# Attention feeding a two-layer network: the down-sampled pairs of later batches get shifted start times

## The chip, the core and the metric

The kernel runs on one NeuronCore of one Trainium2 chip. Five engines work from their own queues, each in program order: TensorE (PE in the profile; PEld is its weight load), VectorE (DVE), ScalarE (ACT), GpSimd (POOL) and SyncE (SP), which here only issues transfers. They wait for one another through semaphores. Matrix products land in PSUM, which has eight banks of 128 partitions by 512 float32 values. The metric is the device time of one execution in microseconds. The kernel before takes 1014.43 us, the median of three runs (1014.23, 1014.43 and 1015.88).

## The reference, cut to what matters

For 8 batches of 8 heads with 576 tokens of 64 values there are two attentions: one over tokens averaged by fours (144 of them), whose rows are repeated four times, and a local one in which a token sees only the tokens less than four places away. Their sum is the input of a network with 2048 hidden units.

```python
q_d, k_d, v_d = (z.reshape(B, H, Sd, 4, D).mean(axis=3) for z in (q, k, v))
out_up = np.repeat(sm_attn(q_d, k_d, v_d), 4, axis=2)
mask = np.abs(pos[:, None] - pos[None, :]) < 4
scores = np.where(mask, scale * (q @ k.T), -1e9)
attn_out = out_up + softmax(scores) @ v          # (8, 8, 576, 64)
x = attn_out.transpose(0, 2, 1, 3).reshape(4608, 512)
h = x @ w_in                                      # (4608, 2048)
out = (np.maximum(h, 0) + alpha * np.minimum(h, 0)) @ w_out
```

## The kernel before, in words

The network is the larger part. Its 4608 rows are cut into 18 chunks of 256, and the 2048 hidden units into 8 blocks of 256, which makes 144 steps. One step s is `hidden` (24 products into `h`, line 752), then `slopes` (two pairs of ACT operations, lines 760 and 761), `larger` (one DVE maximum, line 764) and `split` (ACT makes the upper part `gh`, line 769, POOL the rest `gl`, line 69), and then `product` (12 products into `o`, line 798). Operands stand as an upper and a lower part, so each product is made of three.

The attention of the first batch is worked out ahead of all that. The other seven batches run beside the network. Their local attention comes in units, three to a batch (u = 3 to 23), and is DVE work for the most part: `multiply` and `total` (lines 591 and 595), a softmax, then `weigh` and `gather` (lines 647 and 650). At the end of a unit, `flip` turns its result on PE (`xp`, line 659) in two parts, and `join` (DVE, line 671) reads that, adds the down-sampled result and so frees the bank; `place` makes the network's operands `xh` and `xl` of it.

The down-sampled attention comes in pairs of heads, four to a batch, each handled by one call of `down`. A pair is a chain on several engines. Its six inputs are loaded (`load`, line 232, through SP's queue into a ring of three tiles `ld`) and summed by fours (`fold`, line 238, POOL). Then `flip` turns the sums on PE (`qkT`, line 250); `operands` copies them out (ACT, `qd` and `kd`, lines 255 and 258); `scores` (PE, `s`, line 263); `peak` (DVE, `dnb`, line 267) and `exps` (ACT, `dp`, line 273); `invert` and `scale`; two `turn`s (PE, `pT`, line 287) with two `turned` (ACT, `th`, line 291); `weigh` (PE, `pv`, line 297) and `store` (ACT, `od`, line 302).

Five results of a pair (`qkT`, `s`, two `pT`, `pv`) and the two `xp` of a unit live in one PSUM pool of two banks, `bank("d")`, defined at line 62. A new one can be written only when the last reader of what stood in its bank is done. I call the time from the write to that last read a stay.

No scheduler orders the work. Each operation is entered with a due time counted in network steps (`at`), and all entries are sorted by that time; ties keep the order of entry. Step s enters `hidden` at s - 1.95, `slopes` at s - 1.45, `larger` at s - 1.15, `split` at s - 1.0 and `product` at s + 0.6. A pair that is entered with `t0` and a gap of 0.45 folds at t0, t0 + 0.45 and so on, and flips at t1 = t0 + 3.0; the rest follows at the offsets of line 312: operands at t1 + 0.5, scores at 1.0, peak at 1.6, exps at 1.7, the turns at 3.0, weigh at 4.0, store at 4.5. A unit u starts at begin[u], and units are 5.92 steps apart after the first few. Lines 891 to 894 enter the pairs of batches 2 to 7, evenly spread over three units of time. They come ahead of the units, whose flips depend on places inside their own lists. I write "pair 4_3" for batch 4, pair 3, "u11_1" for part 1 of unit 11, and h62 and p62 for `hidden` and `product` of step 62.

Of the kernel before, what the change touches and what calls it, by code (L numbers as in the profile page):

```python
# [16 lines left out]
B, H, S, D = 8, 8, 576, 64  # L17
# [33 lines left out]
def tile_attention_moe(ctx: ExitStack, tc: tile.TileContext, q, k, v, w_in, w_out, alpha, out):  # L51
# [514 lines left out]
    def local(u, t0, t1):  # L566
        b, jj = u // 3, u % 3
# [118 lines left out]
                at_ += n  # L686

        def put(i, t):
            at(t, join, i)
            at(t + 0.05, place, i, False)  # L690
            at(t + 0.3, place, i, True)
# [21 lines left out]
        t = t0  # L713
        when = {}
# [18 lines left out]
            at(when["total", str((1, 5, 2))] + 0.05, load_kv, u + 1, "k")  # L733
            at(t1 + 0.05, load_kv, u + 1, "v")
        if by_half:
            at(when["own"] - 0.6, flip, 0)
            put(0, when["own"])
        return when, put, flip


# [92 lines left out]
    with tc.tile_pool(name="start", bufs=1) as start:  # L833
        load_pair, load_windows, pair = first_batch(start)
        todo = [(w, fp) for fp in range(NP) for w in range(2)]
        for step in ORDER.split():
            kind, i = step[0], int(step[1])
# [16 lines left out]
        def at(t, f, *args):  # L854
            events.append((t, len(events), f, args))
# [19 lines left out]
    t = T0_DEC  # L875
# [7 lines left out]
    for p in range(4 * (B - 1)):  # L883
        b, hp = 1 + p // 4, p % 4
# [3 lines left out]
    begin = dict(UNITS)  # L888
    for u in range(len(UNITS) + 3, 3 * B + 1):
        begin[u] = begin[u - 1] + U_STEP  # L890
    for b in range(2, B):
        first, end = begin[3 * b - 2], begin[3 * b + 1]
        for hp in range(4):
            down(b, hp, first + (end - first - 0.5) * hp / 4 - (2.7 if b == 2 else 4.5), 0.45)
    at(3.3, load_q, 3)
    at(3.4, load_kv, 3, "k")
    at(decoded + 0.3, load_kv, 3, "v")
    at(decoded + 0.6, place_rest)
    put = None
    for u in range(3, 3 * B + 1):  # L900
        if u < 3 * B:
            when, *mine = local(u, begin[u], begin[u + 1])
        else:
            when = {"before 0": begin[u] + 0.8, "before 1": begin[u] + 1.2}
        if put and u - 1 in BY_HALF:
            at(begin[u] + 0.3, flip, 1)
            put(1, when["before 0"])
        elif put:
            at(begin[u] + 0.3, flip, 0)
            put(0, when["before 0"])  # L910
            t = when["before 0"] + 0.25 if u == 4 else when["before 1"]
            at(max(begin[u] + 0.31, t - 0.6), flip, 1)
            put(1, t)
        put, flip = mine
    with tc.manual_schedule():
        for _, _, f, args in sorted(events, key=lambda e: e[:2]):
            f(*args)
# [25 lines left out]
```

## Time and profile before

| what | value |
|---|---|
| median of three runs | 1014.43 us |
| the profiled execution | 1012.62 us |
| its span, first to last instruction | 1010.8 us |
| mean granted TensorE clock | 0.973 |
| DVE busy | 832.8 us (82%) |
| POOL busy | 482.1 us (48%) |
| PE idle of its span | 50.2 us |

The span is 1.82 us shorter than the execution's own time. The chain of waits is the work that ended last, followed back from the last instruction. In a table of stretches, each row gives the busy time of the engines between two times of the span, with the number of their instructions, then the granted clock, the share of the DMA engines that was busy and what they moved. In a timeline, a row gives start, length, engine, line, operation, output and inputs, and in brackets how long the engine had been idle before it and what released it.

### The profile page before, as it was taken

To read this page: it belongs to the slowest core of one execution; us is meant where nothing else is said; L and a number is where in the kernel's file an instruction comes from. 1 tells how busy PE (TensorE), PEld (TensorE's weight loads), DVE (VectorE), ACT (ScalarE), POOL (GpSimd) and SP (SyncE) were. 2 spreads that over 40 slices of the span, in tenths; PEclk is the share of its full clock that TensorE was granted. 3 is DMA by queue.
4 is the path that set the end of the run, shared out by engine and by line. 5 is a ranking of instruction groups with operands and counts; after the bars stand their busy time and mean duration, and the time that the engine had idled before them with its cause. 6 is when DMAs were issued, how large, how long until landed. Compare 5 with 4: busy or idle time off the path is not lost.

```text
span 1010.8 us, 17864 instructions
## 1 busy us (share of the span) xinstructions
PE 960.6 (95%) x6402; PEld 852.7 (84%) x6402; DVE 832.8 (82%) x1347; ACT 560.2 (55%) x1483; POOL 482.1 (48%) x612
## 2 busy tenths in 40 slices
PE   5877989999999999999999999999999999999998
PEld 4756878898888898988888888888988898989997
DVE  6899988899888899899888898898898899997111
ACT  4767766465565555555455555555555554444442
POOL 2040645677665546555554544656555543323221
PEclk9856989999999999999999999999999999999999
DMA  8946443232422322433322332322331412210000
GB/s 191 222 148 242 123 153 98 83 119 83 145 83 73 118 81 78 121 97 93 103 88 66 100 111 71 125 80 74 123 100 60 131 49 61 86 43 22 1 21 22
DMA packets 61218, 98.26 MB, mean 97 GB/s; under 512 B 21578, under 2 KB 26954, under 8 KB 61130
## 3 DMA queue, kind: packets, MB, share of 16 engines
q1 hardware_dynamic: 60938, 96.87, 32.0%
q8 instruction: 50, 0.82, 0.3%
q10 hardware_dynamic: 192, 0.26, 0.1%
q14 instruction: 38, 0.31, 0.1%
HBM read 87.67 MB, written 9.44 MB: 96 GB/s over the span
## 4 chain that ended last, share of the span: by engine, by line
PE 72%; DVE 15%; ACT 4%; issue 3%; DMA 2%; POOL 2%; SPq 2%; DVEq 0%; ACTq 0%; POOLq 0%
PE o L798 33%; PE h L752 33%; DMA raw<-in_moe_w_out 2%; DVE qk L591 2%; DVE lb L650 2%; PE s L263 2%; DVE t L764 1%; PE pv L297 1%; DVE ls L595 1%; DVE temp L193 1%; DVE pv L647 1%; PE xp L659 1%; PE pT L287 1%; DVE temp L194 1%; DMA ld<-in_q 1%
## 5 line engine op out<-in xcount | busy, mean ns | idle before, releaser
L69 POOL TENSOR_TENSOR gl<-t,gh 128x512 fp32r<-128x512 f32 x144 | 186.5, 1295 | 390.8 <-ACT gh L769 347.4
L760 ACT ACTIVATE t<-h,slope 128x256 f32<-128x256 f32 x288 | 136.3, 473 | 203.0 <-PE h L752 166.2
L764 DVE TENSOR_TENSOR t<-h,t 128x512 f32<-128x512 f32 x144 | 99.0, 687 | 113.2 <-ACT h L761 108.6
L752 PE MATMUL h<-xh,wih 128*128 128x256 f32 x1152 | 190.9, 287 | 0.7 <-ACT xh L518 0.7
L798 PE MATMUL o<-woh,gh 128*128 128x512 f32 x576 | 188.1, 407 | 0.4 <-ACT woh L203 0.4
L752 PE MATMUL h<-xl,wih 128*128 128x256 f32 x1152 | 183.7, 281 | 0.6 <-POOL xl L69 0.6
L752 PE MATMUL h<-xh,wil 128*128 128x256 f32 x1152 | 184.1, 282 | 0.0
L798 PE MATMUL o<-wol,gh 128*128 128x512 f32 x576 | 182.1, 397 | 0.1
L798 PE MATMUL o<-woh,gl 128*128 128x512 f32 x576 | 182.1, 397 | 0.0
L752 PEld LDWEIGHTS h<-xh,wih 128*128 128x128 f32 x1152 | 163.5, 190 | 10.5 <-issue 1.8
L72 POOL TENSOR_TENSOR ld<-ld 72x256 f32<-72x256 f32 x168 | 125.4, 747 | 73.9 <-DMA ld<-in_q 49.4
L752 PEld LDWEIGHTS h<-xl,wih 128*128 128x128 f32 x1152 | 156.9, 190 | 0.8 <-POOL xl L69 0.8
L752 PEld LDWEIGHTS h<-xh,wil 128*128 128x128 f32 x1152 | 157.3, 190 | 0.0
L769 ACT CAST gh<-t 128x512 fp32r<-128x512 f32 x144 | 89.1, 619 | 118.7 <-DVE t L764 68.4
L595 DVE TENSOR_REDUCE ls<-qk 128x12 f32<-128x768 f32 (+1 forms) x126 | 136.4, 1083 | 2.8
L798 PEld LDWEIGHTS o<-woh,gl 128*128 128x128 f32 x576 | 108.6, 189 | 26.4
L798 PEld LDWEIGHTS o<-wol,gh 128*128 128x128 f32 x576 | 108.4, 188 | 26.4 <-DVE wol L211 0.7
L761 ACT ACTIVATE h<-h,sign 128x256 f32<-128x256 f32 x288 | 126.4, 439 | 0.0
L650 DVE TENSOR_TENSOR lb<-lb,pv 128x384 f32<-128x384 f32 x202 | 113.9, 564 | 5.5
L798 PEld LDWEIGHTS o<-woh,gh 128*128 128x128 f32 x576 | 98.3, 189 | 16.3 <-issue 2.2
L647 DVE TENSOR_TENSOR pv<-v,lb 128x1152 f32<-128x1152 f32 x84 | 93.6, 1115 | 2.6
L591 DVE TENSOR_TENSOR qk<-k,qp 128x768 f32<-128x768 f32 (+1 forms) x78 | 84.0, 1077 | 0.0
(148 smaller groups left out, 1111.4 us busy)
## 6 DMA issues: line engine op xcount, KB each, us to landing
k<-in_k SPq DMA_DIRECT2D x41, 384.0 KB
v<-in_v SPq DMA_DIRECT2D x41, 384.0 KB
raw<-in_moe_w_in SPq DMA_DIRECT2D x16, 512.0 KB
raw<-in_moe_w_out SPq DMA_DIRECT2D x16, 512.0 KB
ld<-in_q SPq DMA_DIRECT2D x56, 144.0 KB
ld<-in_k SPq DMA_DIRECT2D x56, 144.0 KB
ld<-in_v SPq DMA_DIRECT2D x56, 144.0 KB
q<-in_q SPq DMA_DIRECT2D x42, 192.0 KB
```

The source lines that it names most:

```text
L69: nc.gpsimd.tensor_tensor(o, a, b, op=ALU.subtract)
L72: nc.gpsimd.tensor_tensor(o, a, b, op=ALU.add)
L591: nc.vector.tensor_tensor(st["pr"][:, :nd], window(tiles[u, "k"], half, d0, nd), st["qp", half].unsqueeze(1).to_broadcast([128, nd, 2, 192 ...
L595: nc.vector.tensor_reduce(out=st["s"][:, half, d0:d0 + nd, :].rearrange("p a b -> p (a b)"), in_=st["pr"][:, :nd].rearrange("p a h (t d) - ...
L647: nc.vector.tensor_tensor(st["pr"][:, :nd], window4(tiles[u, "v"], half, d0, nd), prob(half, d0, nd), op=ALU.mult)
L650: nc.vector.tensor_tensor(st["acc"], st["acc"], st["pr"][:, i], op=ALU.add)
L752: nc.tensor.matmul(ph[:, j], w[:, m, 128 * o:128 * o + 128], x[:, m, :], start=(i == 0), stop=(i == 11))
L760: nc.scalar.activation(t[:, j], hs[st][:, j], AF.Copy, scale=slope[:, f:f + 1])
L761: nc.scalar.activation(hs[st][:, j], hs[st][:, j], AF.Copy, scale=sign[:, f:f + 1])
L764: nc.vector.tensor_tensor(gs[st], hs.pop(st), gs[st], op=ALU.max)
L769: nc.scalar.copy(gh, t)
L798: nc.tensor.matmul(outs[c][m], g[:, j, 128 * m:128 * m + 128], wo[w][n][:, o, :], start=(f == 0 and i == 0), stop=(f == NF - 1 and i == 2))
```

## The change

The units are entered first. While that is done, `put` and the new `flip_at` record for every part of a unit a stay from its flip to 0.3 steps after its join. Then, pair by pair, the code tries 29 shifts from -0.7 to +0.7 steps in steps of 0.05. For each it takes the pair's five stays at fixed lengths (0.65 for `qkT`, 0.85 for `s`, 0.55 and 0.59 for `pT`, 0.65 for `pv`), sorts them among all stays so far, and sums by how much a stay ends after the start of the next but one. The shift with the smallest sum is taken, of those the one nearest to zero, and the pair is entered there, loads, folds and all.

```diff
         def put(i, t):
+            stays.append((when_flipped[u, i], t + 0.3))
             at(t, join, i)
...
-    for b in range(2, B):
-        first, end = begin[3 * b - 2], begin[3 * b + 1]
-        for hp in range(4):
-            down(b, hp, first + (end - first - 0.5) * hp / 4 - (2.7 if b == 2 else 4.5), 0.45)
...
+    stays, when_flipped = [], {}
+
+    def flip_at(u, i, t, flip):
+        when_flipped[u, i] = t
+        at(t, flip, i)
...
+    def stays_of(t1):
+        return [(t1 + a, t1 + z) for a, z in ((0, 0.65), (1.0, 1.85), (3.0, 3.55), (3.01, 3.6), (4.0, 4.65))]
+
+    def late_by(mine):
+        order = sorted(stays + mine)
+        return sum(max(0.0, a[1] - c[0]) for a, m, c in zip(order, order[1:], order[2:]) if {a, m, c} & set(mine))
+
+    for b in range(2, B):
+        first, end = begin[3 * b - 2], begin[3 * b + 1]
+        for hp in range(4):
+            t0 = first + (end - first - 0.5) * hp / 4 - (2.7 if b == 2 else 4.5)
+            shift = min((0.05 * k for k in range(-14, 15)), key=lambda x: (round(late_by(stays_of(t0 + x + 3.0)), 2), abs(x)))
+            stays += stays_of(t0 + shift + 3.0)
+            down(b, hp, t0 + shift, 0.45)
```

At the unit's own flips `at(t, flip, i)` becomes `flip_at(...)` with the same times. The shifts that come out are, for pairs 0 to 3 of each batch: batch 2: 0.70, 0.55, -0.70, 0; batch 3: -0.05, -0.70, 0, -0.45; batch 4: 0, -0.15, 0.05, -0.60; batch 5: 0.45, -0.15, 0.05, -0.60; batch 6: 0, -0.70, 0.55, 0; batch 7: 0, -0.70, 0, -0.45. Seven pairs stay where they were. No instruction is added or removed; line numbers from 689 on grow by one and more.

Four places follow. In the rows the first number after a name's underscore is the pair, the number at the end a buffer's.

PE behind h62, before: the second part of u11 is flipped, then both turns of pair 4_3, then p60 begins.

```order
L752 MATMUL h_6016<-xl_4792,wih_1257 128x256 x4
L659 MATMUL xp_1_6041<-ident,x_5664 128x128 x2
L287 MATMUL pT_3_0_6044<-ident,dp_3_5935 72x96 x3
L287 MATMUL pT_3_1_6050<-ident,dp_3_5935 72x96 x3
L798 MATMUL o_0_5759<-woh_889,gh_5940 128x512
```

The same place after the change, from the end of p59 on.

```order
L799 MATMUL o_1_5760<-woh_841,gl_5865 128x512
L287 MATMUL pT_3_0_5999<-ident,dp_3_5901 72x96 x3
L287 MATMUL pT_3_1_6003<-ident,dp_3_5901 72x96 x3
L753 MATMUL h_6023<-xh_4791,wih_1257 128x256 x4
L753 MATMUL h_6023<-xh_4791,wil_1258 128x256 x4
L753 MATMUL h_6023<-xl_4792,wih_1257 128x256 x4
L753 MATMUL h_6023<-xh_4791,wih_1257 128x256 x4
L753 MATMUL h_6023<-xh_4791,wil_1258 128x256 x4
L753 MATMUL h_6023<-xl_4792,wih_1257 128x256 x4
L659 MATMUL xp_1_6048<-ident,x_5666 128x128 x2
L799 MATMUL o_0_5759<-woh_889,gh_5939 128x512
```

The two turns moved to the other side of h62, ahead of the unit's flip.

ACT at step 28, before: the slopes of h28, then the cast of `split`, then the copies that read `qkT` of pair 3_0.

```order
L760 ACTIVATE t_3341<-h_3294,slope 128x256
L761 ACTIVATE h_3294<-h_3294,sign 128x256
L769 CAST gh_3374<-t_3341 128x512
L255 ACTIVATE qd_84<-qkT_0_3333 64x3x48 x2
L258 COPY kd_0_3380<-qkT_0_3333 128x144
L291 COPY th_3_0_3411<-pT_3_0_3366 72x288
```

The same place after the change.

```order
L761 ACTIVATE t_3343<-h_3296,slope 128x256
L762 ACTIVATE h_3296<-h_3296,sign 128x256
L255 ACTIVATE qd_84<-qkT_0_3337 64x3x48 x2
L258 COPY kd_0_3370<-qkT_0_3337 128x144
L770 CAST gh_3380<-t_3343 128x512
L291 COPY th_3_0_3418<-pT_3_0_3372 72x288
```

The copies `qd` and `kd` moved ahead of the cast `gh`: the pair moved by 0.05 steps, and its `operands` from 27.0, where `split` is due too, to 26.95.

PE behind h32, before: `pv` of pair 3_0 and the second part of u6; `qkT` of pair 3_1 stands twelve products further on, behind p30.

```order
L752 MATMUL h_3628<-xl_2902,wih_80 128x256 x4
L297 MATMUL pv_0_3658<-th_0_0_3619,s2v_0_3239 64x144 x2
L297 MATMUL pv_0_3658<-th_0_1_3621,s2v_0_3239 64x144 x2
L659 MATMUL xp_1_3668<-ident,x_3319 128x128 x2
L798 MATMUL o_0_3183<-woh_1529,gh_3549 128x512
```

The same place after the change.

```order
L753 MATMUL h_3630<-xl_2911,wih_80 128x256 x4
L250 MATMUL qkT_1_3655<-ident,s2q_1_3411 128x72 x2
L250 MATMUL qkT_1_3655<-ident,s2k_1_3469 128x72 x2
L297 MATMUL pv_0_3663<-th_0_0_3620,s2v_0_3239 64x144 x2
L297 MATMUL pv_0_3663<-th_0_1_3623,s2v_0_3239 64x144 x2
L659 MATMUL xp_1_3673<-ident,x_3321 128x128 x2
L799 MATMUL o_0_3184<-woh_1529,gh_3554 128x512
```

Now `qkT` of pair 3_1 comes first, `pv` and `xp` behind it, all between h32 and p30. By the bank numbers in the built program, `qkT` and `xp` share a bank here.

PE behind p20 after the change, the end of p20 and the start of h23. Behind h22, one product block earlier, `s` of pair 2_2 has just been written; `pv` of pair 2_1 goes into the same bank.

```order
L799 MATMUL o_0_2471<-woh_889,gl_2681 128x512
L799 MATMUL o_1_2472<-woh_889,gl_2681 128x512
L659 MATMUL xp_0_2838<-ident,x_2725 128x128 x3
L297 MATMUL pv_1_2842<-th_1_0_2806,s2v_1_2393 64x144 x2
L297 MATMUL pv_1_2842<-th_1_1_2808,s2v_1_2393 64x144 x2
L753 MATMUL h_2858<-xh_1734,wih_1257 128x256 x4
```

Before the change `xp_0` stood there alone: `pv` of pair 2_1 stood behind h22, together with `qkT` of pair 2_2, and `s` of pair 2_2 behind h23.

More of the change, by code (lines that the diff above doesn't have):

```diff
@@ L735, in local @@
         if by_half:
-            at(when["own"] - 0.6, flip, 0)
+            flip_at(u, 0, when["own"] - 0.6, flip)
             put(0, when["own"])
@@ L905, in tile_attention_moe @@
         if put and u - 1 in BY_HALF:
-            at(begin[u] + 0.3, flip, 1)
+            flip_at(u - 1, 1, begin[u] + 0.3, flip)
             put(1, when["before 0"])
         elif put:
-            at(begin[u] + 0.3, flip, 0)
+            flip_at(u - 1, 0, begin[u] + 0.3, flip)
             put(0, when["before 0"])
             t = when["before 0"] + 0.25 if u == 4 else when["before 1"]
-            at(max(begin[u] + 0.31, t - 0.6), flip, 1)
+            flip_at(u - 1, 1, max(begin[u] + 0.31, t - 0.6), flip)
             put(1, t)
         put, flip = mine
+    def stays_of(t1):
[10 more added lines that the diff above has]
+            down(b, hp, t0 + shift, 0.45)
     with tc.manual_schedule():
```

## The prediction, made before the changed kernel had run

> **What bounds the kernel now.** I read the page first, then a table of stretches, then PE's waits in the stretch that the change touches.
>
> ```profile
> span 1010.8 us, 17864 instructions
> PE 72%; DVE 15%; ACT 4%; issue 3%; DMA 2%; POOL 2%; SPq 2%; DVEq 0%; ACTq 0%; POOLq 0%
> 190.00:870.00 680.00, 667.73 (x4501) 596.56 (x4500) 602.19 (x972) 377.95 (x1042) 372.75 (x473) 1.00 0.30 93
> 870.00:1000.00 130.00, 130.00 (x839) 117.45 (x838) 63.31 (x102) 57.56 (x129) 36.83 (x31) 1.00 0.09 25
> ```
>
> The chain that ended last is PE work for 72%. The stretch rows have PE, PEld, DVE, ACT and POOL busy, then the granted clock. The pairs of batches 2 to 7, the only ones moved, write PSUM from 187 us to about 845 us. In 190 to 870 PE is busy for 667.7 of 680 us at full clock, DVE for 602.2. So PE sets the pace, and at most its 12.3 us of idle time can be won; before 190 us and behind 870 us nothing moves. The waits in that stretch:
>
> ```profile
> PE pT L287 <- DVE lb L616: 2.5, 1, 2.5
> PE pT L287 <- DVE xf L671: 2.2, 2, 1.5
> PE pT L287 <- ACT th L291: 2.1, 2, 1.7
> PE xp L659 <- ACT kd L258: 1.7, 1, 1.7
> PE qkT L250 <- ACT od L302: 1.6, 2, 1.4
> PE pT L287 <- ACT kd L258: 1.2, 1, 1.2
> PE h L752 <- POOL xl L69: 0.6, 1, 0.6
> PE xp L659 <- ACT th L291: 0.2, 1, 0.2
> ```
>
> All but the `xl` row are writes into the two-bank pool, and they end when a reader of the same bank ends (the 2.5 is credited to a later DVE row; the last `join` had just ended). One of them in full:
>
> ```profile
> 283.68 0.62 ACT L769 CAST gh<-t 128x512 fp32r<-128x512 f32 x1 [1.40 <-PE o L798]
> 284.21 0.57 ACT L255 ACTIVATE qd<-qkT 64x144 f32<-64x144 f32 x2
> 284.79 0.28 ACT L258 COPY kd<-qkT 128x144 f32<-128x144 f32 x1
> 285.13 0.44 PE L287 MATMUL pT<-ident,dp 96*72 96x96 f32 x3 [1.24 <-ACT kd L258]
> ```
>
> `qkT` of pair 3_0 was copied out only behind the cast `gh`, until 285.07; the second `pT` of pair 2_3 started at 285.13 in that bank. These ten waits make 11.5 us, the `xl` wait 0.6: 12.1 us in all.
>
> **What goes.** Following the order of the changed program, I looked for each of the ten. The `xp` of u3 at 192.5 us no longer has `qkT` of 2_0 between its parts (1.7). Both `pT` of 2_2, of 4_3, of 5_0, of 5_3 and of 6_2 no longer stand directly by an `xp` (the first three rows, 6.8). The copies of 3_0 now precede `gh` (1.2): without the cast's 1.40 us of idle time and its 0.53 they would end at 283.1, and PE wanted the bank at 285.13 - 1.24 = 283.9. `qkT` of 6_2 and 7_1 and the `xp` of u16 leave their neighbours (1.8). In each case one whole block of 12 or 24 products or more now lies between the last write of the bank and the next: 2.9 us, where the copy of `qkT` that is worked out below needs 2.7. So I take all 11.5 us off.
>
> **What comes.** I listed in the new order every write with at most one block between it and the last write of its bank. Most have 3 us of products and a copy of some 2 us to cover. Two do not.
>
> *The second part of u6 behind `qkT` of pair 3_1, after h32.* The rows from before show the pace of such small groups, and of ACT behind h32:
>
> ```profile
> 239.23 0.29 PE L250 MATMUL qkT<-ident,s2q 72*128 72x72 f32 x2
> 239.57 0.71 PE L297 MATMUL pv<-th,s2v 72*64 72x144 f32 x8
> 240.21 0.73 PE L798 MATMUL o<-woh,gh 128*128 128x512 f32 x2
> 243.11 0.49 PE L659 MATMUL xp<-ident,x 128*128 128x128 f32 x3
> 243.35 0.72 PE L752 MATMUL h<-xh,wih 128*128 128x256 f32 x4
> 246.24 0.90 PE L263 MATMUL s<-kd,qd 128*96 128x144 f32 x6
> 246.88 0.72 PE L798 MATMUL o<-woh,gh 128*128 128x512 f32 x2
> 307.77 0.71 PE L297 MATMUL pv<-th,s2v 72*64 72x144 f32 x8
> 307.94 0.47 ACT L760 ACTIVATE t<-h,slope 128x256 f32<-128x256 f32 x1 [2.79 <-PE h L752]
> 309.16 0.44 ACT L761 ACTIVATE h<-h,sign 128x256 f32<-128x256 f32 x1
> ```
>
> Start to start, `qkT` takes 0.34 us, `pv` 0.64, a product block 2.90, a three-part `xp` 0.24, an `h` block 2.89, `s` 0.64. With h32 done at 307.77, PE would reach the `xp` at 307.77 + 0.34 + 0.64 = 308.75. ACT runs the four slope operations first, until 309.60, then `qd` (0.57) and `kd` (0.28), so it ends at 310.45. The wait is **1.7 us**. The chain is fixed by program order, so it isn't under 1.5; with one cast (0.62) in front it would be 2.3. Behind it stand p30 and all of PE's later work.
>
> *`pv` of pair 2_1 behind `s` of pair 2_2, after p20.* Here the readers are `peak` on DVE and then three exponentials on ACT. In the new order of DVE, `peak` stands behind `larger` of step 22 and one `multiply`. From before:
>
> ```profile
> 242.87 0.68 DVE L764 TENSOR_TENSOR t<-h,t 128x512 f32<-128x512 f32 x1
> 243.47 0.94 DVE L591 TENSOR_TENSOR qk<-k,qp 128x768 f32<-128x768 f32 x1
> 248.01 0.60 DVE L267 TENSOR_REDUCE dnb<-s 96x3 f32<-96x432 f32 x1
> 249.01 0.37 ACT L273 ACTIVATE dp<-s,dnb 96x144 f32<-96x144 f32 x1
> 249.72 0.38 ACT L273 ACTIVATE dp<-s,dnb 96x144 f32<-96x144 f32 x1
> ```
>
> h22 ended at 239.23. `larger` started at 242.87 because DVE was behind, not idle. The `multiply` ends at 244.41, `peak` at about 245.0, the exponentials (249.01 to 250.10, so 1.09) at about 246.1. PE needs 239.23 + 0.64 + 2.90 + 0.24 = 243.01 to reach `pv`. The wait is **3.1 us**. If DVE were not behind, `larger` would start at about 241.1 as soon as the slopes are done, and the wait would be 1.3; with one more `multiply` of 0.94 ahead it would be 4.0. Program order excludes a wait below zero. I take 3.1, since DVE's load ahead of that point hardly changes. This wait comes just before h23, so it also gives POOL time for the `xl` that h24 waited for: the 0.6 goes.
>
> A third place is near its limit: the second part of u12 stands two blocks behind `s` of 5_0, whose read takes about as long; I take 0.3, with 0 and 2 as ends. The other such places get 0 to 2 together, taken as 0, since each has 0.5 us or more to spare by the reads of before.
>
> **The clock.** PE's clock fell to half in two windows of 3.41 us, each behind a window with a wait:
>
> ```profile
> 139.50:142.91 3.41, 1.71 (x18) 1.00 0.16 43
> 142.91:146.32 3.41, 3.41 (x18) 0.50 0.12 43
> 141.21 0.34 PE L250 MATMUL qkT<-ident,s2q 72*128 72x72 f32 x2 [1.70 <-ACT th L291]
> 143.59 1.05 PE L752 MATMUL h<-xl,wih 128*128 128x256 f32 x4
> 144.45 1.05 PE L752 MATMUL h<-xh,wih 128*128 128x256 f32 x4
> 525.20:532.00 6.80, 4.31 (x33) 1.00 0.53 168
> ```
>
> In 139.50 to 142.91 PE was idle for 1.70 us and did a good us of transposes and small products, and the next window ran at 0.50: groups of four products came every 0.86 us instead of 2.89 / 6 = 0.48. That costs 3.41 x (1 - 0.48 / 0.86) = 1.5 us. The wait of 2.5 us near 529 did not do it; the clock stayed at 1.00, its idle time being split between two windows. The new places have 0.24 + 3.1 + 0.64 = 4.0 us and 0.34 + 0.64 + 1.7 = 2.7 us without dense products, both more than 139.50 had. Whether each does it depends on where it falls on the window grid. I count one half-clock window, **1.5 us**, with ends 0 and 4.5.
>
> The Trainium skill, "TensorE: Matmul & The Clock Gate", section "HAM oscillation — how this bites in real kernels", puts the limit at idle gaps of over about 3.4 us. By that rule neither new wait would slow the clock and the sum would be 1.5 us better. The trace speaks against it: 1.70 us of idle time in a window was enough at 141 us.
>
> **The sum.** -12.1 + 1.7 + 3.1 + 0.3 + 1.5 = **-5.5 us**. The profiled execution took 1012.62 us, so it would take 1007.1. The median of the runs shown is 1.81 us above it; from there, 1014.43 - 5.5 = **1008.9 us**. The same PE work remains: small groups stand at 136 places between blocks instead of 132, and none is added.
>
> On the other queues, all six loads and folds of a pair move with it. On SP the loads of 2_2 are now all due before the `v` of u5, whose issue moves from 221.0 us to about 223.7; DVE wants it at 232.4, so it is hidden with some 5 us to spare. If that cover fails it costs DVE up to 3 us. On POOL the first fold of 2_2 is now due before the flip of 2_1, whose sums it overwrites; POOL has 372.75 busy of 680 us, and `gl` is used over a step later.
>
> **The rivals.** *The clock holds.* Neither new place covers enough of a window. Speaks for it: 525.20:532.00 above. Then -12.1 + 5.1 = -7.0, so 1007.4. It is also the case that the rule of the Trainium skill gives.
>
> *VectorE takes over.* DVE has only 680 - 602.2 = 77.8 us of idle time in the stretch, and near 240 us it was already 1.8 us behind. PE, once it waits less, could meet late `join`s and `larger`s instead, and give most of it back: about 4 us, so 1012.9, within 0.2%. Against: away from 190 to 270 us DVE has some 12% idle, and a PE that waits in one spot usually found the reader late only there.
>
> *The readers are late more often (slower).* The new order keeps 25 writes with at most one block between them and the last write of their bank, against 22 before. The row of `gh` above shows the mechanism: copies that stand behind a cast end 1.4 us later. A block of 2.9 us then no longer covers them, and each such place costs some 1.2 us and, with the clock, up to 1.5 more. With more than two such places (2 x 2.7 = 5.4) the gain is gone; with four, -5.5 + 10.8 = +5.3, and the time is 1019.7. Against: I placed each copy in the new order, and only the two above came out late.
>
> *It doesn't do what it says.* The fixed lengths aren't the real stays (the read of `s` takes about 6 us above, a whole step). The overlap then moves rather than goes; the two new waits are this rival in part, and more of it is the case before.
>
> **How the numbers follow.** Forecast 0.60, clock holds 0.20, VectorE 0.12, late readers 0.08. A measurement tells about 0.2% (2 us) from no change. So faster 0.80, same 0.12, slower 0.08. The range takes in the forecast's ends (lower: waits of 1.5 and 1.3 and no clock loss, -12.1 + 2.8, so 1005.1; upper: 2.3, 4.0, 2, 2 and 4.5, +2.7, which all at once is unlikely) and the VectorE case: 1004.5 to 1013.
>
> **What would show it.** Right: PE's waits in 190 to 870 us fall to about 5 us, with a wait of `xp` on `kd` of 1.7 us near 305 us, one of `pv` on `dp` near 240 us, and no `pT` row over 0.5 us; one half-clock window behind one of them. Wrong: waits of PE on `t` or `h` (VectorE), or more than three waits of a bank's writes over 1 us (late readers), or PE's waits down by more than 10 us (the two costs were mistaken).

## The result and the profile after

The changed kernel takes **1009.48 us**, the median of five runs (1008.81 to 1010.72); the kernel before took 1014.43 us in five runs beside it (1012.40 to 1015.88). The ratio is 0.9946, with a 95% interval of 0.9923 to 0.9968: faster by half a per cent, 5.0 us, where 5.5 was forecast. The profiled execution of the changed kernel took 1008.81 us, with a span of 1006.8.

The page of the changed kernel has the same PE work in a shorter span, and the chain that ended last goes through PE for 82% instead of 72%.

```profile
span 1006.8 us, 17856 instructions
PE 82%; DVE 9%; ACT 3%; issue 2%; SPq 2%; DMA 1%; POOL 1%; ACTq 0%; POOLq 0%; DVEq 0%
```

The same two stretches of the changed kernel (columns as before: PE, PEld, DVE, ACT and POOL busy, granted clock, DMA share, GB/s):

```profile
190.00:870.00 680.00, 674.78 (x4540) 605.18 (x4540) 608.65 (x977) 380.11 (x1048) 375.85 (x477) 0.99 0.31 94
870.00:1000.00 130.00, 130.00 (x828) 116.92 (x827) 60.08 (x99) 56.64 (x127) 36.83 (x31) 1.00 0.08 25
```

PE's idle time in the first stretch fell from 12.3 to 5.2 us. But the mean clock of the stretch, 1.00 before, is 0.99; where it fell is shown below. PE's waits between 190 and 1000 us are down to three rows:

```profile
PE pv L297 <- ACT dp L273: 2.9, 1, 2.9
PE xp L659 <- ACT kd L258: 1.7, 1, 1.7
PE xp L659 <- DVE xf L671: 0.6, 1, 0.6
```

None of the eight rows of before is left as it stood: the `xp` on `kd` has the same name and size, but it stood at 192.5 us and now stands at 312.5. The first two rows are the two places that were named beforehand. The first in full, from the timeline of the changed kernel (start, length, engine, line, operation, output and inputs, and in brackets the idle time before it and its releaser):

```profile
243.14 0.49 PE L659 MATMUL xp<-ident,x 128*128 128x128 f32 x3
243.17 0.68 DVE L765 TENSOR_TENSOR t<-h,t 128x512 f32<-128x512 f32 x1
243.77 0.94 DVE L591 TENSOR_TENSOR qk<-k,qp 128x768 f32<-128x768 f32 x1
244.63 0.59 DVE L267 TENSOR_REDUCE dnb<-s 96x3 f32<-96x432 f32 x1
245.26 0.38 ACT L273 ACTIVATE dp<-s,dnb 96x144 f32<-96x144 f32 x1 [0.70 <-DVE dnb L267]
245.99 0.37 ACT L273 ACTIVATE dp<-s,dnb 96x144 f32<-96x144 f32 x1
246.50 0.51 PE L297 MATMUL pv<-th,s2v 72*64 72x144 f32 x2 [2.87 <-ACT dp L273]
```

`peak` of pair 2_2 (`dnb`) waits on DVE behind `larger` and a `multiply`, its exponentials on ACT wait for it, and PE stands still for 2.87 us until the last of them has freed the bank. The second place, from the same view:

```profile
309.99 0.48 ACT L761 ACTIVATE t<-h,slope 128x256 f32<-128x256 f32 x1 [2.78 <-PE h L753]
311.57 0.58 ACT L255 ACTIVATE qd<-qkT 64x144 f32<-64x144 f32 x2
312.15 0.28 ACT L258 COPY kd<-qkT 128x144 f32<-128x144 f32 x1
312.49 0.44 PE L659 MATMUL xp<-ident,x 128*128 128x128 f32 x2 [1.70 <-ACT kd L258]
```

Four slope operations, two copies, then `xp`. The clock, in single windows of 3.41 us around the first place:

```profile
242.68:246.09 3.41, 0.95 (x6) 0.57 (x4) 3.40 (x5) 1.45 (x6) 1.45 (x2) 1.00 0.03 4
246.09:249.51 3.42, 3.01 (x16) 2.62 (x17) 2.78 (x12) 1.59 (x7) 1.51 (x3) 0.50 0.78 270
249.51:252.92 3.41, 3.41 (x18) 3.41 (x17) 0.00 (x0) 0.00 (x0) 3.33 (x6) 0.50 0.00 0
252.92:256.33 3.41, 3.41 (x20) 2.88 (x19) 1.33 (x3) 3.10 (x9) 0.96 (x2) 1.00 0.15 43
```

Two windows ran at 0.50, not one. The wait ended 0.41 us into the first of them, so that one wasn't full either, and the clock came back only behind a window in which PE was busy throughout. One execution of each kernel was traced; what the clock cost in its other executions isn't shown.

### The profile page after: what moved, and what is told of

Read it like the earlier page. It is cut to its first block, busy times and chain, and to the rows that moved or that the text cites. A ratio compares the mean times of both kernels' runs of the same rounds, so it can differ in the third digit from the quotient of the medians.

```text
span 1006.8 us, 17856 instructions
## 1 busy us (share of the span) xinstructions
PE 962.7 (96%) x6402; PEld 856.1 (85%) x6402; DVE 833.5 (83%) x1347; ACT 561.1 (56%) x1483; POOL 485.0 (48%) x612
## 4 chain that ended last, share of the span: by engine, by line
PE 82%; DVE 9%; ACT 3%; issue 2%; SPq 2%; DMA 1%; POOL 1%; ACTq 0%; POOLq 0%; DVEq 0%
PE h L753 38%; PE o L799 37%; PE pv L297 2%; PE s L263 2%; PE xp L659 1%; PE pT L287 1%; DVE temp L193 1%; DVE temp L194 1%; DMA raw<-in_moe_w_in 1%; SPq L393 1%; ACT temp L184 1%; DVE temp L188 1%; PE qkT L250 1%; DVE t L765 1%; DVE temp L189 1%
## 5 line engine op out<-in xcount | busy, mean ns | idle before, releaser
L761 ACT ACTIVATE t<-h,slope 128x256 f32<-128x256 f32 x288 | 136.9, 475 | 192.5 <-PE h L753 161.4
L753 PE MATMUL h<-xh,wih 128*128 128x256 f32 x1152 | 192.5, 289 | 0.7 <-ACT xh L518 0.7
```

What stands on the lines that cost most here:

```text
L753: nc.tensor.matmul(ph[:, j], w[:, m, 128 * o:128 * o + 128], x[:, m, :], start=(i == 0), stop=(i == 11))
L761: nc.scalar.activation(t[:, j], hs[st][:, j], AF.Copy, scale=slope[:, f:f + 1])
```

## The experiments

All of them start from the changed kernel. I keep one account of every trace: the time from the first product of h14 to the last product of the network, less PE's idle time there (gaps over 0.04 us), and less 0.44 us for each microsecond at half clock (0.44 is 1 - 0.48 / 0.86, the two paces that the prediction read from the rows). If waits and clock are the whole story, what is left must be the same in all kernels.

| kernel | h14 to the end | PE's waits | at half clock | left over | ratio to before | its interval |
|---|---|---|---|---|---|---|
| before | 822.39 | 12.27 | 0 | 810.12 | 1 | |
| changed | 816.59 | 5.21 | 6.83 | 808.38 | 0.9946 | 0.9923 to 0.9968 |
| e1_weigh_later | 812.42 | 3.64 | 0 | 808.78 | 0.9908 | 0.9891 to 0.9925 |
| e2_both_apart | 810.72 | 1.93 | 0 | 808.79 | 0.9888 | 0.9868 to 0.9907 |
| e5_none_left | 809.13 | 0.52 | 0 | 808.61 | 0.9873 | 0.9853 to 0.9893 |
| e3_batch2_back | 815.78 | 5.47 | 3.41 | 808.80 | 0.9948 | 0.9928 to 0.9967 |
| e4_only_batch2 | 826.41 | 12.00 | 10.24 | 809.90 | 1.0019 | 0.9999 to 1.0039 |
| e6_longer_s | 819.76 | 7.95 | 6.83 | 808.81 | 0.9993 | 0.9976 to 1.0009 |
| e7_peak_earlier | 814.47 | 4.18 | 3.41 | 808.79 | one run | |
| e8_30_unshifted | 819.60 | 6.43 | 10.24 | 808.66 | one run | |

What is left is the same, to 0.4 us, in the eight kernels in which most or all of batches 3 to 7 are shifted, though the time itself varies by over 10 us. In the two in which they are not (before and e4), 1.1 to 1.7 us more are left over; 0.7 of the 1.7 comes back behind the last product (4.1 us from there to the end of the span before, 4.8 in the changed kernel). The rest, up to about a microsecond, I have not traced. The account takes idle time inside a slow window off twice. Where it counts once (0.41 us in the changed kernel, 0.40 in e4, 0.22 in e8), the eight agree to 0.25 us (808.56 to 808.81) and the other two to 0.05 (810.12 and 810.07), so the difference between the two groups is real: waits and clock are nearly the whole story, not all of it.

### Taking the new waits away one by one

**e1_weigh_later** moves `pv` of pair 2_1 behind the next block, away from `s` of pair 2_2:

```diff
-                              (4.0, weigh), (4.5, store)):
+                              (4.2 if (b, hp) == (2, 1) else 4.0, weigh), (4.5, store)):
```

> The changed kernel with one entry moved: the weighing of pair 2_1 is due 0.2 steps later, so that its write to PSUM stands behind h23 instead of ahead of it. Theory (PE sets the time; it loses what its own waits last, plus what the half clock behind a wait costs): the wait of pv on dp (2.9 us) goes, the half-clock stretch of 6.8 us behind it goes too (3.0 us), and the xl wait of h24 (0.6 us) comes back: 5.3 us less than the changed kernel, a profiled span of about 1001.5 us, a ratio of 0.990 to the kernel before. Rival 1 (VectorE takes over): the idle time turns up again as PE waits for h or late joins, and less than 2 us is won (ratio 0.993 or more). Rival 2 (the half clock there has nothing to do with the wait): the half-clock stretch stays and 2.3 us is won (0.9925).

It took 1003.98 us (median of 6), ratio 0.9908, where 0.990 was expected. Its waits:

```profile
PE xp L659 <- ACT kd L258: 1.7, 1, 1.7
PE h L753 <- POOL xl L69: 1.3, 1, 1.3
PE xp L659 <- DVE xf L671: 0.6, 1, 0.6
```

The 2.9 is gone, and with it both half-clock windows; between 190 and 999 us the clock never fell. The wait of h24 on `xl`, which the changed kernel didn't show, is back, at 1.33 us instead of the 0.59 of before. So the wait of `pv` had covered it: removing 2.87 us of waiting won 1.57 us of waiting and 3.0 us of clock.

**e2_both_apart** also enters the second flip of u6 a little later, so that the block of p30 stands between `qkT` of pair 3_1 and it:

```diff
-        at(t, flip, i)
+        at(t + (0.03 if (u, i) == (6, 1) else 0.0), flip, i)
```

> As the run with the later weighing, and the second part of u6 is flipped 0.03 steps later, behind p30 instead of ahead of it. Theory: the wait of xp on kd (1.7 us) goes as well, so 7.0 us less than the changed kernel, a span of about 999.8 us, a ratio of 0.988 to the kernel before; PE's waits between 190 and 870 us are then at most some 1.5 us. Rival (VectorE takes over): the join of u6 comes later and PE waits for it or for later maxima; no gain over the run with the later weighing alone.

1001.97 us (median of 6), ratio 0.9888, where 0.988 was expected. The 1.7 is gone; 1.3 (`xl`) and 0.6 (`xf`) are left, 1.9 us together where at most some 1.5 was expected.

**e5_none_left** takes these two as well, by entering `place` of u5's first part 0.05 steps earlier and the first `join` of u4 0.25 earlier:

```diff
-            at(t + 0.3, place, i, True)
+            at(t + (0.25 if (u, i) == (5, 0) else 0.3), place, i, True)
...
-            put(0, when["before 0"])
+            put(0, when["before 0"] - (0.25 if u == 5 else 0.0))
```

> As the run with both places apart, and the two waits that it has left are gone after too: the first join of u4 is due 0.25 steps earlier, and POOL makes the xl of u5 0.05 steps earlier, ahead of its far products. Theory: PE waits less than 0.3 us from 190 to 1000 us, 1.9 us less than the run with both places apart, ratio 0.987 to the kernel before. Rival (VectorE takes over once PE no longer waits): the waits come back under other names on DVE or POOL, no gain over that run.

**1001.75 us** (median of 5), ratio 0.9873, the lowest ratio of the study: 12.5 us below the 1014.21 of the kernel before in the runs beside it. The ratios of this kernel and of the changed one lie 0.0073 apart, 7.4 us. Against e2 the times decide nothing: the medians are 0.2 us apart and the intervals overlap. It is the trace that shows the gain over e2, 1.6 us in the second column of the account, where 1.9 was expected. Its first stretch, and its only wait over 0.2 us:

```profile
190.00:870.00 680.00, 679.48 (x4587) 609.04 (x4587) 614.72 (x992) 383.73 (x1057) 378.87 (x480) 1.00 0.31 96
```

```profile
PE pv L297 <- ACT dp L273: 0.4, 1, 0.4
```

PE is busy for 679.48 of 680 us at full clock, while DVE has 65 us to spare. The case in which VectorE becomes the bound is excluded by this: with PE busier in this stretch than in any other kernel here, no wait on DVE's `join` or `larger` is left. The 0.4 us is a wait on ACT; PE's idle time makes 0.52 us in all, a little over the 0.3 expected.

**e7_peak_earlier** is a half step at the first place: `peak` and `exps` of pair 2_2 are entered earlier, so that `peak` stands ahead of `larger` and the `multiply` in DVE's queue and the exponentials ahead of the cast `gh` in ACT's. (The diff shows the head of the list of offsets.)

```diff
-        for lag, f, *args in ((0, flip), (0.5, operands), (1.0, scores), (1.6, peak), (1.7, exps), (2.3, invert),
+        for lag, f, *args in ((0, flip), (0.5, operands), (1.0, scores), (1.38 if (b, hp) == (2, 2) else 1.6, peak), (1.42 if (b, hp) == (2, 2) else 1.7, exps), (2.3, invert),
```

> The changed kernel with the readers of s of pair 2_2 due earlier: its peak ahead of the maximum of step 22 on DVE, its exponentials ahead of the cast gh on ACT. PE's order is the same. Theory (the read of s was late because of what stands ahead of it on DVE): the wait of pv falls from 2.9 to about 1.5 us, and the place then has 2.4 us without dense products instead of 3.8, so at most one half-clock window. Rival (the wait is set by PE or by the bank itself): 2.9 us as before.

The one run took 1007.39 us. The wait fell from 2.87 to 1.39 us, and no half clock followed it. So it is indeed what stands ahead of the readers in their queues that makes it. Both readers moved here, so the run alone doesn't part DVE's share from ACT's; in the changed kernel ACT stood idle for 0.70 us until `peak` was done (the row at 245.26 above), so there DVE's queue ended last. `xl` came back with 0.5, and the clock fell once at another place, behind the unchanged wait of u6 (below).

### Undoing the change by batches

**e3_batch2_back** leaves batch 2 where it was, **e4_only_batch2** moves it alone:

```diff
-            down(b, hp, t0 + shift, 0.45)
+            down(b, hp, t0 + (0.0 if b == 2 else shift), 0.45)
```

```diff
-            down(b, hp, t0 + shift, 0.45)
+            down(b, hp, t0 + (shift if b == 2 else 0.0), 0.45)
```

> The changed kernel with the pairs of batch 2 entered without their shifts; those of batches 3 to 7 are shifted as in the changed kernel. Theory: the waits of the kernel before at 192 and 261 us come back (some 2.1 and 1.5 us, and 0.6 for xl), the waits of pv (2.9) and of xp on xf (0.6) and the half clock (3.0) go, the wait of xp on kd near 312 us (1.7) stays: 2.3 us less than the changed kernel, ratio 0.993 to the kernel before. Rival (the shifts of batch 2 carry a share of the gain): slower than the changed kernel, ratio above 0.9965.

> The changed kernel with the pairs of batches 3 to 7 entered without shifts; only batch 2 is shifted. Theory: against the kernel before, 1.7 + 1.5 + 0.6 us of waits go, and 2.9 + 0.6 us of waits and 3.0 us of half clock come: 2.7 us slower than before, ratio 1.003, with the waits of 2.5, 1.7, 1.4, 1.2 and 0.8 us between 285 and 765 us as before. Rival (no wait matters by itself, the clock or VectorE sets the pace): within 0.5 us of the kernel before.

With batches 3 to 7 alone the ratio is 0.9948 (1008.74 us, median of 6), the same as with all of them, where 0.993 was expected. With batch 2 alone it is 1.0019, no gain; its interval holds both the 1.003 expected and no change. Its runs scatter from 1011.01 to 1021.25, and why is not shown. So the gain is that of the later batches. The shifts of batch 2 remove 1.7, 1.5 and 0.6 us of waits, bring 2.9 and 0.7, and bring the clock's loss on top.

The waits of e3 came out nearly as expected (1.7 twice, 1.5, 0.6; the first of them had been put at some 2.1). What was not expected is one half-clock window behind u6's wait of 1.69 us, which had not cost any clock in the changed kernel. It takes 1.5 of the 2.3 us by which e3 was to be faster than the changed kernel:

```profile
308.28:311.69 3.41, 1.72 (x19) 1.38 (x18) 2.79 (x5) 2.56 (x8) 0.00 (x0) 1.00 0.35 105
311.69:315.10 3.41, 3.41 (x10) 2.64 (x9) 0.73 (x3) 0.00 (x0) 0.00 (x0) 0.50 0.57 212
```

The same wait in the changed kernel fell across two windows. The one that held most of it:

```profile
310.95:314.36 3.41, 1.87 (x9) 1.60 (x10) 2.09 (x6) 1.64 (x6) 0.00 (x0) 1.00 0.75 259
```

And in e4 the old wait of 2.4 us near 529 us, which cost no clock before, fell into one window and did:

```profile
525.78:529.19 3.41, 1.00 (x7) 0.59 (x6) 2.69 (x7) 1.90 (x6) 2.35 (x3) 1.00 0.49 167
529.19:532.60 3.41, 3.39 (x17) 3.41 (x18) 2.68 (x7) 1.01 (x3) 2.63 (x5) 0.50 0.56 184
```

### One shift alone

**e8_30_unshifted** sets only the shift of pair 3_0 back, from -0.05 to 0, so that its copies stand behind the cast `gh` again:

```diff
-            down(b, hp, t0 + shift, 0.45)
+            down(b, hp, t0 + (0.0 if (b, hp) == (3, 0) else shift), 0.45)
```

> The changed kernel with pair 3_0 entered without its shift of -0.05 steps, so that its two copies stand behind the cast gh on ACT again. Theory: a single wait of pT on kd of 1.2 to 1.3 us comes back near 285 us, nothing else changes. Rival (so small a shift does nothing): no such wait.

The wait of `pT` on `kd` is back, 1.25 us at 291.8 us, and the others are unchanged. The one run took 1014.89 us, far more than 1.2 above the changed kernel. The account says why: h14 began at 188.47 us instead of 185.41, ahead of anything that the edit touches (3.1), and the clock fell once more behind u6 (3.41 x 0.44 = 1.5). With the wait these make 5.8 of the 6.1 us between the two spans. A single run can't price such an edit; its wait in the trace can.

### Truer lengths for the planner

**e6_longer_s** lets the planner reckon with longer stays for `qkT` and `s`, as the traces show them to be, and choose all shifts anew:

```diff
-        return [(t1 + a, t1 + z) for a, z in ((0, 0.65), (1.0, 1.85), (3.0, 3.55), (3.01, 3.6), (4.0, 4.65))]
+        return [(t1 + a, t1 + z) for a, z in ((0, 0.9), (1.0, 2.1), (3.0, 3.55), (3.01, 3.6), (4.0, 4.65))]
```

> The changed kernel with two of its fixed stay lengths nearer to what the traces show: 0.9 for qkT and 1.1 for s (2.1 instead of 1.85). Pair 2_2 then goes the other way (+0.7), 2_3 by 0.45, and some others by a tenth or two. Theory (the length put in for s let the wait of pv in): the wait of pv on dp (2.9) and the half clock behind it (3.0) go; the wait of xp on kd (1.7) stays, since 3_1 still takes its largest shift; s of 3_0 directly behind a pT of 2_3 in the same bank is new, 1.6; xl of h24 0.6 to 1.3: 2.4 to 3.1 us less than the changed kernel, ratio 0.992. Rival (the lengths don't matter, the room for shifts is too small): the wait of pv stays or as much comes elsewhere, 0.995 as the changed kernel.

This missed: 1013.4 us (median of 10), ratio 0.9993 with 0.9976 to 1.0009, where 0.992 was expected. The wait of `pv` on `dp` is gone, but two others came, the first two rows of its waits. That of `s` had been foreseen, at 1.6 us, and took 2.92; that of `xp` on `od` had not:

```profile
PE s L263 <- ACT th L291: 2.9, 1, 2.9
PE xp L659 <- ACT od L302: 2.7, 1, 2.7
PE xp L659 <- ACT kd L258: 1.7, 1, 1.7
PE xp L659 <- DVE xf L671: 0.7, 1, 0.7
```

Its timeline at the two places:

```profile
244.91 0.62 ACT L770 CAST gh<-t 128x512 fp32r<-128x512 f32 x1 [3.89 <-DVE t L765]
245.44 0.27 ACT L302 COPY od<-pv 128x144 f32<-128x144 f32 x1
245.76 0.65 PE L659 MATMUL xp<-ident,x 128*128 128x128 f32 x3 [2.66 <-ACT od L302]
...
289.64 0.47 ACT L761 ACTIVATE t<-h,slope 128x256 f32<-128x256 f32 x1 [2.70 <-POOL gl L69]
291.21 0.69 ACT L291 COPY th<-pT 72x288 f32<-72x288 f32 x2
291.66 0.61 PE L263 MATMUL s<-kd,qd 128*96 128x144 f32 x3 [2.92 <-ACT th L291]
```

Both readers are short copies (0.27 us, and 0.69 us for two together) that stand behind operations of the network on ACT, and the first of those had itself waited, 3.89 us for DVE and 2.70 for POOL. This is the late-reader mechanism of the prediction's third rival. A stay's length is not a property of the result; it depends on what stands ahead of the reader, and the planner's lengths hold none of that. One pair of lengths doesn't show that truer ones are worse in general. The clock was expected to hold, but two windows ran at half, one behind the first place and one behind u6.

The clock behind the first place adds to the account of the two-window loss. Here the wait ended at 245.76, ahead of the window's start, and a single window ran at half:

```profile
246.08:249.49 3.41, 3.41 (x19) 3.41 (x17) 3.03 (x12) 1.23 (x5) 2.16 (x4) 0.50 0.69 225
249.49:252.91 3.42, 3.42 (x21) 2.97 (x21) 0.38 (x1) 1.62 (x4) 3.34 (x5) 1.00 0.13 49
```

## Why the prediction was right, step by step

- **What bounds it.** Right. PE's idle time was the limit of the gain at the places that move: e5, which has almost none left, ends 12.5 us below before, where 12.3 us of idle time stood.
- **The ten two-bank waits go (11.5 us).** Right as a whole: none of them is in the trace. e3 and e4 show that those of the later batches carry the gain.
- **u6's second part (1.7 us).** Right in place, size and cause: 1.70 us at 312.49, and e2 removes it by one block of distance.
- **`pv` of pair 2_1 (3.1 us).** Right in place and cause, 2.87 us of idle time. The prediction reckoned from 0.24 us behind the start of `xp`; so counted it is 243.14 + 0.24 to 246.50, 3.12 us. The difference is only that a trace counts idle time from the end of the operation before. e7 halved the wait by moving `peak` in DVE's queue and the exponentials in ACT's.
- **The wait on `xl` is covered (0.6 us).** Right: it comes back as soon as the wait of `pv` goes, with 1.33 us in e1.
- **0.3 us at u12.** Wrong place: nothing is seen there. One of the places that were taken as 0 gave 0.64 us instead, the second part of u4 at 227.31 us, behind a late `join`. The new waits together are 5.2 us, where 5.1 were forecast; that the sum is so close is in part luck, since 0.64 us at one place stands for 0.3 at another and `pv` came out 0.24 us shorter as idle time.
- **The clock (1.5 us).** The mechanism is right, the count was not: two windows in a row ran slow, 6.83 x 0.44 = 3.0 us. The prediction had taken one window for each wait that falls badly. Where the wait reached some tenths of a microsecond into the slow window, a second slow one followed: in the changed kernel, e4 and e8 the wait at the first place ended 0.41, 0.38 and 0.22 us into it. In e6, whose wait ended 0.3 us ahead of it, one window was all. The small `pv` products also stood in the slow window of the three, 1.16 us of it, and not in that of e6. That they do it is less likely: e7's slow window at 143.41 us held 1.13 us of `pv` and no idle time, and full clock followed. The prediction also put both new places above the window at 139.50 in time without dense products; that window had 1.70 + 1.04 = 2.74 us, so u6's place, with 2.7, was not above it.
- **What the sum left out.** From before to after the waits make -7.1 us, the clock +3.0, the part that is left over -1.7, the tail +0.7, and h14 began 1.1 us later. That is -4.0, the difference of the spans; the medians differ by -5.0. So the forecast of -5.5 was close in part by luck: the clock cost 1.5 us more than its term, and the -1.7 and +0.7, which the prediction didn't have, made up for two thirds of that. The start varies from run to run: in six of these kernels that do not differ ahead of it (changed, e1, e2, e5, e7, e8), h14 began between 185.1 and 188.5 us.
- **The rivals.** The clock did not hold; e1 shows what that case is worth. VectorE did not take over (e5). Readers were late more often only in e6, where another set of shifts gave the same result as no change. And the change does what it says in part: it takes away the neighbours it can see, and puts new ones in place, two of which cost 4.6 us of waits.

## What to carry to other kernels

In a program whose order is fixed, two writes into the same bank need a block between them that is longer than the reader's whole queue, not than the read: look up what stands ahead of the reader on its engine and what that waits for. When a change removes many small waits and adds one of 3 us, look at that one first: undoing it by moving one operation by 0.2 steps was worth some 4 us (3.8 by the ratios, 4.2 by the account), nearly as much as the whole change. Keep one account for all traces (time less idle less slow clock): where it gives the same remainder each time, waits and clock explain the differences, and where it doesn't, as in the two kernels with 1.3 us more, something else is at work.

## What the hardware showed that was not expected

Whether a wait costs clock depends on where it falls on a grid of 3.41 us that doesn't follow the program. u6's wait of 1.69 to 1.70 us is the same in six kernels:

| kernel | the wait | the window | network products in it | next window |
|---|---|---|---|---|
| changed | 310.79 to 312.49 | 310.95 to 314.36 | 1.68 us | full |
| e1 | 306.32 to 308.01 | 306.78 to 310.19 | 1.99 us | full |
| e3 | 309.59 to 311.28 | 308.28 to 311.69 | 0.47 us | half |
| e6 | 312.20 to 313.89 | 310.93 to 314.35 | 0.47 us | half |
| e7 | 307.85 to 309.54 | 307.25 to 310.66 | 0.92 us | half |
| e8 | 315.36 to 317.05 | 314.17 to 317.59 | 0.47 us | half |

The fourth column is the time in the window that products into `h` and `o` took, from the timeline, each counted from its start to the start of the next operation. Over all ten traces between 190 and 990 us, nine windows were followed by a fall of the clock, and held 0.02 to 0.92 us of such products; the full windows with the least that were not held 0.90, 1.05 and 1.21 us.

That is no rule, for ahead of 190 us the same traces break it. The kernel before lost the clock behind a window with 1.1 us of network products and 0.86 us of transposes, and e4 kept it behind one with 0.90 and 0.86; in the rows PE is busy for 1.98 us in the one and 1.75 us in the other:

```profile
132.67:136.08 3.41, 1.98 (x11) 1.47 (x12) 2.30 (x6) 2.72 (x7) 1.17 (x2) 1.00 0.52 145
136.08:139.50 3.42, 3.42 (x9) 2.08 (x7) 3.35 (x6) 1.70 (x4) 3.11 (x4) 0.50 0.11 37
```

```profile
495.06:498.47 3.41, 1.75 (x18) 1.54 (x17) 2.58 (x7) 1.94 (x5) 2.25 (x4) 1.00 0.71 233
498.47:501.89 3.42, 3.42 (x20) 2.88 (x19) 2.56 (x8) 1.49 (x4) 0.23 (x1) 1.00 0.25 88
```

The changed kernel lost it behind 1.40 us of network products and nothing else (136.87 to 140.28 us). So what decides between two such windows stays open.

The way back asks for more: windows at half clock with 1.85, 1.87 and 2.04 us of network products stayed slow, those with 3.02 and 3.41 us did not. The three also held 0.22 to 0.41 us of idle time and the others at most 0.02, so it can be the idle time as well. These figures are of these kernels alone.

PE's busy share alone does not decide it either. Near 529 us the kernel before had a full window with less PE work than the one of e3 that lost the clock (1.72 us busy):

```profile
525.20:528.61 3.41, 1.63 (x9) 1.08 (x8) 2.00 (x5) 2.22 (x6) 2.29 (x3) 1.00 0.42 125
```

Of its 1.63 us, 1.21 were network products; in e3's window 0.47 of the 1.72 were, 0.54 were transposes and 0.71 the small `pv` products. The Trainium skill, "TensorE: Matmul & The Clock Gate", section "Part 4: PE-mode transpose", says that transposes don't count as busy for the clock in the same way; these two windows agree with it, though the `pv` products are no transposes. The changed kernel's 1.40 us without transposes, behind which the clock fell, and e4's 0.90 with 0.86 us of them, behind which it held, do not agree. The Trainium skill, section "HAM oscillation — how this bites in real kernels" of the same page, sets the limit at idle gaps of about 3.4 us. Here an idle gap of 1.69 us was enough in e3, with transposes and small products beside it.
